# Turning queries, keys and outputs on the matmul engine instead of with transposing transfers, and three VectorE sums moved

## The chip, the cores and the metric

The kernel runs on one core of one Trainium2 chip. The metric is the device time of one execution in microseconds (us), as the median of several runs. One execution was also recorded by the hardware profiler, and all views quoted below come from that recording.

The engines are named as in the profile: PE is the matmul engine (TensorE) and PEld its weight loads, DVE is VectorE, ACT is ScalarE, POOL is GpSimd, and SP is SyncE, which here only issues transfers. A small q behind a name (SPq, PEq) is that engine's sequencer.

## What is computed

Causal attention with 16 extra "beacon" keys and values ahead of each sequence, followed by two matrix products with a leaky ReLU between them:

```python
B, H, S, D = 8, 8, 576, 64            # beacons: 16; d_model 512, d_ff 2048
k_all = concat([beacon_k, k], axis=2); v_all = concat([beacon_v, v], axis=2)
scores = 1/sqrt(D) * q @ k_all^T       # causal over k, beacons always visible
a = softmax(scores)
attn = a @ v_all
x = attn.transpose(0, 2, 1, 3).reshape(B*S, H*D)      # 4608 tokens x 512
h = x @ w_in                                          # 512 -> 2048
out = maximum(0.01*h, h) @ w_out                      # 2048 -> 512
```

Inputs and output are float32; the kernel's matmuls take bf16.

## The kernel before

**Pairs.** The 64 heads are worked on as 32 pairs `g` of two heads (NG = 32, four pairs to a batch). For a pair the kernel needs q and k with the head dimension on the partitions (tiles `qT`, `kT`, 128 x 576: two heads of 64). It then computes transposed scores on PE into PSUM, exponentials on ACT into `aT`, causal triangles on POOL (L289), and on PE the product with the values, `value` (L359), in two halves. DVE divides by the row sums (L388, L389) and writes `x_nat`, tokens on the partitions. For the first product of the second stage `x_nat` has to be turned again, into `xT`.

**How things are turned.** For the first eight pairs, q and k are turned on PE (`t_q`, L243) and copied from PSUM by DVE or ACT (L249). For pairs 8 to 31, POOL loads q and k with a cast (`load_natural`, L171, tiles `q_nat`, `k_nat`, 96 partitions by 6 blocks of 128), and `turn_pair` turns each with one transposing transfer issued by SP (L179). The outputs of pairs 0 to 3, 5, 6, 7 and 31 are turned by `x_transposes` (five PE transposes at L405, one copy at L410). Those of pair 4 and of pairs 8 to 30 are turned by `x_turn`: two or three transposing transfers on SP (L417, L422, L425).

**Second stage.** The 4608 tokens are cut into nine chunks of 512. `moe1` (L442, called by `up`) makes one 128 x 512 block of the hidden layer; ACT applies the leaky ReLU (L450) into `gT`. `moe2` (L525, called by `down`) multiplies by `w_out` in seven products instead of eight (a Strassen-like scheme), each of two tiles of eight matmuls. For these products DVE builds sums of token blocks (`token_sums`, queued in the list `due` and issued one at a time by `add_due`, L801), sums of weight blocks once (`weight_sums`, L468 to L474), and adds the products (L551 for chunk 0, L588 later). The last two chunks also use seven products in the first matrix (`in_round`, L679).

**Order.** Every engine runs its queue in program order, and the order is written by hand. The eight first pairs follow strings of steps given to `run` (for example `T8` turns pair 8, `x7` turns the output of pair 7, `t1` is the second weight sum, `d` is one `down`). From pair 8 (FIRST) on, a list of events with positions in units of a pair is sorted: loads `N` at g - 3.25 and g - 2.95, `T` at g - 1.75, a `block` of scores (three tiles of 512 columns, running over pair limits) every 0.92 units, `value` at g + 2.25 and 0.37 later (0.2 earlier for the last pair of a batch), the turn of the output 0.01 after that. Between the events `fill` issues `up` and `down` so that the work of the second stage is spread evenly.

**PSUM.** Four banks (`ps_one`, tag "one") go round among the `up` blocks, the products of `down`, the value products, the first score tile of a block (two banks) and the tiles `tp` of PE transposes. A bank comes free when ACT or DVE has read it.

Of the kernel before, what the change touches and what calls it, by code (L numbers as in the profile page):

```python
# [9 lines left out]
BF16 = mybir.dt.bfloat16  # L10
# [5 lines left out]
def kernel(  # L16
# [11 lines left out]
    nc = tc.nc  # L28

    B, H, S, D = q.shape  # L30
# [5 lines left out]
    NPAIR = H // 2  # L36
# [9 lines left out]
    NKB = 5  # L46
# [17 lines left out]
    NR = 96  # L64
# [77 lines left out]
    qk_raw, nat, qk = {}, {}, {}  # L142
# [31 lines left out]
            )  # L174
        nat.setdefault(g, []).append(t)

    def turn_pair(g):
        for which, t in enumerate(nat.pop(g)):
            nc.sync.dma_start_transpose(  # L179
                out=operand(g, which).rearrange("c (t r) -> c t r", r=NR),  # L180
                in_=t.rearrange("r t h d -> r (t h d)"),
            )

    def load_beacon_k(b0, b1, eng):
        eng.dma_start(out=bk_raw[:, b0:b1], in_=beacon_k[b0:b1].rearrange("b h n d -> (h n) b d"))
# [33 lines left out]
    def operand(g, which):  # L219
        qk.setdefault(g, [None, None])  # L220
        if which == 0:
            qk[g][0] = headpool.tile([128, S], BF16, name="qT", bufs=5)
            return qk[g][0]
        qk[g][1] = k_bufs[g % NK]
        return qk[g][1][:, NB : NB + S]
# [170 lines left out]
    def x_at(b):  # L396
        assert b < XR or done1[0] >= NF * -(-((b - XR + 1) * S + 48) // 512)
        return b % XR * S
# [10 lines left out]
            )  # L409
        copy(out=xT[:, hp, x_at(b) : x_at(b) + S], in_=ps[:, 0:S])  # L410

    def x_turn(g):
        b, hp = divmod(g, NPAIR)
        x_nat, _ = xs.pop(g)
        t1 = NKB if b < B - 1 else NKB - 1
        dst = xT[:, hp, x_at(b) : x_at(b) + 112 + (t1 - 1) * 128]
        nc.sync.dma_start_transpose(  # L417
            out=dst[:, 112:].rearrange("c (t r) -> c t r", r=128),
            in_=x_nat[:, 1:t1].rearrange("r t e d -> r (t e d)"),
        )  # L420
        if t1 < NKB:
            nc.sync.dma_start_transpose(  # L422
                out=xT[:, hp, x_at(b) + S - 80 : x_at(b) + S], in_=x_nat[0:80, t1].rearrange("r e d -> r (e d)")
            )
        nc.sync.dma_start_transpose(  # L425
            out=dst[:, 0:112], in_=x_nat[0:112, 0].rearrange("r e d -> r (e d)")
        )

    gT = {}

    def moe1(i, fc):
# [30 lines left out]
    def weight_sums(part):  # L462
        b11, b12 = w_out_sb[:, 0:HF, 0:HD], w_out_sb[:, 0:HF, HD:DM]
        b21, b22 = w_out_sb[:, HF:NF, 0:HD], w_out_sb[:, HF:NF, HD:DM]
        t1, t2, t4 = (w_sum[:, i] for i in range(3))
        tt = nc.vector.tensor_tensor
        if part == 0:
            tt(out=t1, in0=b12, in1=b11, op=SUB)  # L468
        elif part == 1:
            tt(out=t2, in0=b22, in1=t1, op=SUB)  # L470
        elif part == 2:
            tt(out=b12, in0=b22, in1=b12, op=SUB)
        else:
            tt(out=t4, in0=b21, in1=t2, op=SUB)  # L474
# [42 lines left out]
    def moe2(i, n2):  # L517
        n, tile = (PRODUCTS if i else FIRST_PRODUCTS)[n2 // 2], n2 % 2
        apart = i == NCH - 1 and n2 >= 10
        if tile == 0 or apart:  # L520
            banks["p"] = one_bank()
        acc = banks["p"]
        lo = 0 if apart else tile * HD
        for fc in range(HF):
            nc.tensor.matmul(  # L525
                out=acc[:, lo : lo + HD],
                lhsT=left(i, n, fc, tile),
                rhs=right(n, fc),
                start=(lo == 0 and fc == 0),
                stop=(fc == HF - 1),  # L530
                skip_group_check=True,
            )
        if apart:
            combine(i, n, acc[:, 0:HD], (tile, tile + 1))
        elif tile == 1:
            (combine if i else combine_first)(i, n, acc, (0, 2))
# [7 lines left out]
    def combine_first(i, n, acc, tiles):  # L544
        def part(name, new=False):
            if new:
                parts[name] = opool.tile([128, 512], FP32, name=name, bufs=1)
            return parts[name]

        def add(to, x, y):  # L550
            nc.vector.tensor_tensor(out=to, in0=x, in1=y, op=ADD)  # L551

        if n in (1, 3, 5):
            nc.scalar.copy(out=part({1: "p1", 3: "p5", 5: "p4"}[n], True), in_=acc)
        elif n == 2:
            add(part("u3", True), acc, part("p1"))
            store(i, 0, 0, tiles, part("u3"))
        elif n == 6:
            add(part("u2", True), acc, part("p1"))
            weight_sums(2)  # L560
        elif n == 7:
            add(part("p1"), acc, part("u2"))
            weight_sums(3)
            p1, p4, p5, u2 = (part(name) for name in ("p1", "p4", "p5", "u2"))

            def rest():
                add(p5, p5, p4)
                add(p5, p5, u2)
                store(i, 0, 1, tiles, p5)
                add(part("u3", True), p1, p4)  # L570
                store(i, 1, 1, tiles, part("u3"))

            late.append((done1[0] + done2[0], rest))
        elif n == 4:
            add_late(True)
            add(part("p4"), acc, part("p1"))
            store(i, 1, 0, tiles, part("p4"))
# [221 lines left out]
    def add_due(n=1):  # L799
        while due and n:  # L800
            nc.vector.tensor_tensor(**due.pop(0)[1])  # L801
            n -= 1

    def add_all(i):
        while due and due[0][0] == i:
            add_due()
# [20 lines left out]
    def down():  # L827
        add_late()
        add_due()
        if at2[1] == 4:  # L830
            add_all(at2[0])
        moe2(*at2)
        done2[0] += 1
        at2[1] += 1
        if at2[1] == ND(at2[0]):
            at2[:] = at2[0] + 1, 0
        turn[0] = 0
# [40 lines left out]
    def run(steps):  # L878
        for step in steps.split():
            op, a = step[0], [int(x) for x in step[1:].split(".")] if step[1:] else []  # L880
            if op == "s":
                score(*a)
            elif op == "m":
                mask(*a)
            elif op == "v":
                value(*a)
            elif op == "e":
                value_ahead(*a)
            elif op == "x":
                finish(*a)  # L890
            elif op == "l":
                load_qk(*a)
            elif op == "V":
                load_v_cast(*a)
            elif op == "N":
                load_natural(*a)
            elif op == "T":
                turn_pair(a[0])
            elif op == "y":
                x_turn(a[0])  # L900
            elif op == "q" or op == "k":
                t_q(a[0], 0 if op == "q" else 1, (dve, act)[a[1] if len(a) > 1 else 0])
            elif op == "b":
                beacon_columns(a[0], (dve, act, pool)[a[1]])
            elif op == "u":
                up()
            elif op == "d":
                down()
            elif op == "w":
                unused(*a)  # L910
            elif op == "W":
                unused_ahead(*a)
            elif op == "i":
                load_w_in(a[0])
            elif op == "o":
                load_w_out(a[0])
            elif op == "t":
                weight_sums(a[0])
            else:
                raise ValueError(step)  # L920
# [11 lines left out]
    with order:  # L932
# [16 lines left out]
        run("w2.384 s1.0 m1.0 q2 s1.1 k2 w2.384 s1.2 m1.1 w2.384 s1.3 m1.2 W0.0.4 s2.0 m2.0 W0.0.4 s2.1 W0.0.6 q3 l5.0 l5.1 s2.2 k3 w4.384 v0.0 m2.1 s2.3 i1 m2.2 W0.1.4 s3.0 m3.0 v1.0 s3.1 v0.1 s3.2 v1.1 m3.1 l6.0 l6.1 s3.3 x0.1 m3.2")  # L949
        run("v2.0 V1.0 V1.1 q4 v2.1 x1 k4.1 v3.0 v3.1 x2.1 s4.0 s4.1 x3 m4.0 V1.2 V1.3 V1.4 l7.0 l7.1 u u s4.2 s4.3 q5 k5 m4.1 m4.2 u o0 u")  # L950
        load_beacon_k(2, B, nc.gpsimd)
        run("s5.0 s5.1 m5.0 u u u s5.2 s5.3 q6 k6 m5.1 m5.2 o1 u u s6.0 s6.1 m6.0 u v4.0 u v4.1 y4 N8.0 N8.1 u s6.2 s6.3 q7 k7 m6.1 m6.2 u")
        cast_beacon_k(2, B, nc.gpsimd.tensor_copy)
        run("u v5.0 u v5.1 N9.0 s7.0 s7.1 m7.0 d x5 v6.0 v6.1 t0 T8 d s7.2 s7.3")
        beacon_transposes(2, B)
        run("m7.1 m7.2 N9.1 u b8.2 b9.2 b10.2 b11.2 x6 v7.0 T9 v7.1 d d d N10.0 N10.1 d V2.0 V2.1 x7 t1 T10")


        FIRST = 2 * NPAIR
# [24 lines left out]
        for g in range(FIRST, NG):  # L984
            if g > FIRST + 2:
                events.append((g - 3.25, 0, run, ("N%d.0" % g,)))
                events.append((g - 2.95, 0, run, ("N%d.1" % g,)))
            if g > FIRST + 2:
                events.append((g - 1.75, 0, run, ("T%d" % g,)))
            if g > FIRST + 3:  # L990
                events.append((g - 2.5, 0, run, ("b%d.2" % g,)))
            at = g + (2.05 if g % NPAIR == NPAIR - 1 else 2.25)
            events.append((at, 3, value, (g, 0)))
            events.append((at + 0.37, 4, value, (g, 1)))
            if g < NG - 1:
                events.append((at + 0.38, 5, x_turn, (g,)))
        for m in range((TILES + 2) // 3):
            events.append((FIRST + (0.4 if m else 0.6) + 1536 / COLS * m, 2, block, (m,)))
        ends = [FIRST]
# [60 lines left out]
```

## Time and profile before

| | |
|---|---|
| time, median of 3 runs | 327.32 us (327.24 to 327.57) |
| profiled execution, its own time | 325.4 us |
| its span, first to last instruction | 323.5 us |
| PE busy | 313.3 us (97%) |
| DVE, ACT, POOL busy | 174.6, 205.1, 186.5 us |
| mean granted PE clock | 0.999 |
| transposing transfers on SP | 24 + 24 (q, k) and 51 (outputs) |

An instruction's line in these views tells engine, source line, operation, the tile written and read, shapes, how often, busy time, mean length, and the idle time of the engine before it with what ended it. Matmuls are pipelined, so the length of one matmul (say 273 ns for 256 columns) is longer than the distance to the next (109 ns); where the cost of a group on PE matters, the distance from its start to the start of the next group is the thing to read.

### The profile page before, as it was taken

What the parts mean: (1) busy time and instruction counts of PE and PEld (TensorE: products, weight loads), DVE (VectorE), ACT (ScalarE), POOL (GpSimd) and SP (SyncE); (2) the same over time, 40 slices, a digit from 0 to 9 for tenths busy, and PEclk for the clock granted to TensorE, in tenths of its full rate; (3) what the DMA queues carried; (4) which work ended last, traced back from release to release, by engine and by line L of the source; (5) the groups of instructions that cost most, each with busy time, mean ns of one, the idle gap of its engine ahead of it and who ended that gap; (6) DMA issues with size and microseconds to landing.
All of it is one profiled execution on the core that took longest, in us unless ns stands there. A gap on an engine that the chain in (4) does not pass through costs nothing.

```text
span 323.5 us, 8812 instructions
## 1 busy us (share of the span) xinstructions
PE 313.3 (97%) x3517; PEld 223.6 (69%) x3542; DVE 174.6 (54%) x352; ACT 205.1 (63%) x349; POOL 186.5 (58%) x354
## 2 busy tenths in 40 slices
PE   8999997989999999999999999999999999999995
PEld 5584576655588557855788888656875688688784
DVE  3473388455355244444543454425464689577954
ACT  4969863569856786478746874687458546455510
POOL 8994979989997787659875977666221000000000
PEclk9999999999999999999999999999999999999999
DMA  8999999999999999999999999999422101200113
GB/s 139 142 209 175 140 202 128 166 142 208 145 137 164 189 179 126 123 179 98 133 167 183 122 120 129 184 140 113 55 76 84 26 0 34 77 23 0 67 65 131
DMA packets 155769, 39.79 MB, mean 123 GB/s; under 512 B 142368, under 2 KB 153504, under 8 KB 155728
## 3 DMA queue, kind: packets, MB, share of 16 engines
q0 software_dynamic: 99824, 18.54, 86.0%
q1 hardware_dynamic: 55632, 20.62, 38.5%
q8 instruction: 27, 0.44, 0.6%
q14 instruction: 14, 0.11, 0.1%
q10 hardware_dynamic: 272, 0.07, 0.1%
HBM read 37.22 MB, written 9.44 MB: 144 GB/s over the span
## 4 chain that ended last, share of the span: by engine, by line
PE 80%; DMA 10%; ACT 3%; DVE 2%; POOL 1%; issue 1%; SPq 0%; ACTq 0%
PE acc L442 26%; PE acc L525 21%; PE sc L525 11%; PE av L359 7%; PE sc L314 5%; DMA kT<-k_nat 5%; PE acc L679 5%; DMA w_out_sb<-in_moe_w_out_dram 4%; PE sc L267 2%; DMA gsum<-in_k_dram 1%; ACT aT L333 1%; PE tp L243 1%; POOL aT L289 1%; ACT aT L276 1%; ACT gT L450 1%
## 5 line engine op out<-in xcount | busy, mean ns | idle before, releaser
L442 PE MATMUL acc<-xT,w_in_sb 128*128 128x512 bf16 (+1 forms) x535 | 116.3, 354 | 1.3
L450 ACT ACTIVATE gT<-acc 128x512 bf16<-128x512 f32 x124 | 70.8, 624 | 33.0 <-PE acc L442 32.6
L289 POOL TENSOR_SCALAR_AFFINE_SELECT aT<-aT 128x256 bf16<-128x256 bf16 (+2 forms) x160 | 61.6, 415 | 51.2 <-ACT aT L329 30.7
L442 PEld LDWEIGHTS <-w_in_sb 128*128 128x128 bf16 x560 | 51.6, 98 | 43.0 <-issue 2.7
L525 PEld LDWEIGHTS <-gT 128*128 128x128 bf16 x576 | 54.6, 98 | 12.0 <-issue 4.0
L333 ACT ACTIVATE aT<-sc 128x1024 bf16<-128x1024 f32 (+3 forms) x64 | 51.7, 891 | 0.0
L388 DVE RECIPROCAL rec<-av 128x6 f32<-128x6 f32 (+1 forms) x64 | 11.9, 186 | 64.8 <-PE av L359 64.3
L525 PEld LDWEIGHTS <-gsum 128*128 128x128 bf16 x432 | 40.9, 98 | 8.4 <-DVE gsum L801 1.2
L329 ACT ACTIVATE aT<-sc 128x512 bf16<-128x512 f32 (+3 forms) x64 | 28.9, 520 | 21.1 <-PE sc L314 20.4
L359 PEld LDWEIGHTS <-aT 128*128 128x128 bf16 (+1 forms) x960 | 36.7, 98 | 7.9 <-issue 0.6
L359 PE MATMUL av<-v_aug,aT 128*128 128x65 bf16 (+1 forms) x960 | 39.0, 194 | 0.0
L525 PE MATMUL acc<-w_out_sb,gT 128*128 128x256 bf16 x288 | 34.9, 273 | 1.2 <-DMA w_out_sb<-in_moe_w_out_dram 0.6
L171 POOL DMA_DIRECT2D k_nat<-in_k_dram x48 | 34.8, 731 | 1.9 <-DMA v_aug<-in_v_dram 0.8
L214 POOL DMA_DIRECT2D v_aug<-in_v_dram x40 | 34.2, 862 | 2.9 <-DMA w_in_sb<-in_moe_w_in_dram 2.8
L171 POOL DMA_DIRECT2D q_nat<-in_q_dram x48 | 34.8, 730 | 0.7 <-issue 0.5
L389 DVE TENSOR_TENSOR x_nat<-av,rec 128x384 bf16<-128x384 f32 (+1 forms) x64 | 31.4, 491 | 2.2
L276 ACT ACTIVATE aT<-sc 128x1024 bf16<-128x1024 f32 (+3 forms) x32 | 25.9, 875 | 1.9 <-PE sc L267 1.9
L525 PE MATMUL acc<-w_sum,gsum 128*128 128x256 bf16 x192 | 23.9, 273 | 0.0
L314 PE MATMUL sc<-qT,kT 64*128 64x80 bf16 (+22 forms) x384 | 22.3, 250 | 0.7 <-DMA kT<-k_nat 0.6
L801 DVE TENSOR_TENSOR gsum<-gT 128x1024 bf16<-128x1024 bf16 x18 | 12.7, 705 | 15.7 <-ACT gT L450 15.7
L314 PEld LDWEIGHTS <-kT 64*128 64x128 bf16 x384 | 12.8, 94 | 11.2 <-issue 7.0
L591 ACT COPY p<-acc 128x512 f32<-128x512 f32 x15 | 9.1, 604 | 16.0 <-PE acc L525 16.0
(98 smaller groups left out, 332.5 us busy)
## 6 DMA issues: line engine op xcount, KB each, us to landing
out_dram<-p SPq DMA_DIRECT2D x25, 256.0 KB, 3.6
q_nat<-in_q_dram POOLq DMA_DIRECT2D x48, 72.0 KB, 5.4
k_nat<-in_k_dram POOLq DMA_DIRECT2D x48, 72.0 KB, 5.4
v_aug<-in_v_dram POOLq DMA_DIRECT2D x24, 128.0 KB, 6.5
out_dram<-u SPq DMA_DIRECT2D x9, 256.0 KB, 4.7
w_in_sb<-in_moe_w_in_dram POOLq DMA_DIRECT2D x2, 1024.0 KB, 12.3
w_out_sb<-in_moe_w_out_dram POOLq DMA_DIRECT2D x2, 1024.0 KB, 11.5
gsum<-in_q_dram POOLq DMA_DIRECT2D x8, 144.0 KB, 6.0
```

The costliest lines, as they stand in the source:

```text
L171: nc.gpsimd.dma_start(out=t[:, :, par], in_=(q, k)[which][b, 2 * hp + par].rearrange("(t p) d -> p t d", p=NR),)
L214: nc.gpsimd.dma_start(out=dst[lo : ROWS[c], c, :, 0:D], in_=v[b, :, OFF[c] : OFF[c] + n].rearrange("h p d -> p h d"),)
L276: nc.scalar.activation(out=aT[:, :, c0 : c0 + w], in_=sc[:, :, 0:w], func=AF.Exp, scale=0.125)
L289: nc.gpsimd.affine_select(out=view, in_=view, compare_op=ALU.is_ge, fill=0.0, base=128 - n if lo == 0 else 0, channel_multiplier=-1, patte ...
L314: nc.tensor.matmul(out=(sc[par] if apart else sc[:, par])[:, at : at + b - a], lhsT=kT[ps_, c * 128 : (c + 1) * 128], rhs=qT[ps_, q0 : q0 ...
L329: nc.scalar.activation(out=probs[g][:, par, lo:hi], in_=sc[par][:, at : at + hi - lo], func=AF.Exp, scale=0.125)
L333: nc.scalar.activation(out=probs[g][:, :, lo:hi], in_=sc[:, :, at : at + hi - lo], func=AF.Exp, scale=0.125)
L359: nc.tensor.matmul(out=avv[:, n, 0 : D + 1], lhsT=aT[0 : ROWS[c], par, a0 : a0 + 128], rhs=va[0 : ROWS[c], c, 2 * hp + par, :], start=(c = ...
L389: nc.vector.tensor_tensor(out=x_nat[:, t0:t1].rearrange("p t e d -> p (t e) d"), in0=avv[:, :, 0:D], in1=rec[:, n0:n1, None].to_broadcast( ...
L442: nc.tensor.matmul(out=acc[:, lo:hi], lhsT=w_in_cols(fc, j), rhs=xT[:, j, x0 : x0 + hi - lo], start=(j == 0), stop=(j == NJ - 1), skip_gro ...
L450: nc.scalar.activation(out=gT[i][:, fc, :], in_=acc, func=AF.Prelu, alpha=0.01)
L525: nc.tensor.matmul(out=acc[:, lo : lo + HD], lhsT=left(i, n, fc, tile), rhs=right(n, fc), start=(lo == 0 and fc == 0), stop=(fc == HF - 1) ...
```

## The change

`turn_pair` and `x_turn` go, and with them all 99 transposing transfers. `turn_natural(g, which)` takes the place of the first: six PE transposes of 96 x 128 into a PSUM bank and one DVE copy into `qT` or `kT`. For the outputs of pair 4 and of pairs 8 to 30 `x_transposes` is used, with the copy on DVE. Positions: `T` is now two events, q at g - 1.15 and k at g - 0.85; the output is turned 0.75 instead of 0.38 units after the first value half. `T8` moves to the end of the strings, `T9` and `T10` into the events. Three sums on VectorE stand earlier: the weight sum of L472 directly behind that of L470 (in `t1`), the weight sum of L474 behind product 6 instead of product 7, and at the second product of chunk 0 two more token sums are issued ahead of the product.

```diff
-    def turn_pair(g):
-        for which, t in enumerate(nat.pop(g)):
-            nc.sync.dma_start_transpose(
-                out=operand(g, which).rearrange("c (t r) -> c t r", r=NR),
-                in_=t.rearrange("r t h d -> r (t h d)"),
+    def turn_natural(g, which):
+        t = nat[g][which]
+        ps = ps_one.tile([128, 1024], BF16, name="tp", tag="one")
+        for n in range(S // NR):
+            nc.tensor.transpose(
+                ps[:, n * NR : (n + 1) * NR], t[:, n].rearrange("r h d -> r (h d)"), ident[0:NR, 0:NR]
             )
+        nc.vector.tensor_copy(out=operand(g, which), in_=ps[:, 0:S])
...
-    def x_turn(g):
...
@@ weight_sums
         elif part == 1:
             tt(out=t2, in0=b22, in1=t1, op=SUB)
-        elif part == 2:
             tt(out=b12, in0=b22, in1=b12, op=SUB)
         else:
             tt(out=t4, in0=b21, in1=t2, op=SUB)
@@ combine_first
         elif n == 7:
             add(part("p1"), acc, part("u2"))
-            weight_sums(3)
@@ down
         if at2[1] == 4:
             add_all(at2[0])
+        elif at2 == [0, 2]:
+            add_due(2)
         moe2(*at2)
@@ the strings of the first pairs
-   ... "v4.0 u v4.1 y4 N8.0 N8.1 u s6.2" ...
+   ... "v4.0 u v4.1 N8.0 N8.1 u x4 s6.2" ...
-   ... "v6.0 v6.1 t0 T8 d s7.2 s7.3"
+   ... "v6.0 v6.1 t0 d s7.2 s7.3"
-   "m7.1 m7.2 N9.1 u b8.2 b9.2 b10.2 b11.2 x6 v7.0 T9 v7.1 d d d N10.0 N10.1 d V2.0 V2.1 x7 t1 T10"
+   "m7.1 m7.2 N9.1 u b8.2 b9.2 b10.2 b11.2 x6 v7.0 v7.1 d d d N10.0 N10.1 d V2.0 V2.1 x7 t1 T8.0 T8.1"
@@ the events
-            if g > FIRST + 2:
-                events.append((g - 1.75, 0, run, ("T%d" % g,)))
+            if g > FIRST:
+                events.append((g - 1.15, 0, run, ("T%d.0" % g,)))
+                events.append((g - 0.85, 0, run, ("T%d.1" % g,)))
...
-                events.append((at + 0.38, 5, x_turn, (g,)))
+                events.append((at + 0.75, 5, x_transposes, (g, dve)))
```

More of the change, by code (lines that the diff above doesn't have):

```diff
@@ L410, in x_transposes @@
         copy(out=xT[:, hp, x_at(b) : x_at(b) + S], in_=ps[:, 0:S])
-    def x_turn(g):
[L413 to L427, printed above, removed]
     gT = {}
@@ L897, in run @@
             elif op == "T":
-                turn_pair(a[0])
-            elif op == "y":
-                x_turn(a[0])
+                turn_natural(*a)
             elif op == "q" or op == "k":
@@ L951 @@
         load_beacon_k(2, B, nc.gpsimd)
-        run("s5.0 s5.1 m5.0 u u u s5.2 s5.3 q6 k6 m5.1 m5.2 o1 u u s6.0 s6.1 m6.0 u v4.0 u v4.1 y4 N8.0 N8.1 u s6.2 s6.3 q7 k7 m6.1 m6.2 u")
+        run("s5.0 s5.1 m5.0 u u u s5.2 s5.3 q6 k6 m5.1 m5.2 o1 u u s6.0 s6.1 m6.0 u v4.0 u v4.1 N8.0 N8.1 u x4 s6.2 s6.3 q7 k7 m6.1 m6.2 u")
         cast_beacon_k(2, B, nc.gpsimd.tensor_copy)
-        run("u v5.0 u v5.1 N9.0 s7.0 s7.1 m7.0 d x5 v6.0 v6.1 t0 T8 d s7.2 s7.3")
+        run("u v5.0 u v5.1 N9.0 s7.0 s7.1 m7.0 d x5 v6.0 v6.1 t0 d s7.2 s7.3")
         beacon_transposes(2, B)
-        run("m7.1 m7.2 N9.1 u b8.2 b9.2 b10.2 b11.2 x6 v7.0 T9 v7.1 d d d N10.0 N10.1 d V2.0 V2.1 x7 t1 T10")
+        run("m7.1 m7.2 N9.1 u b8.2 b9.2 b10.2 b11.2 x6 v7.0 v7.1 d d d N10.0 N10.1 d V2.0 V2.1 x7 t1 T8.0 T8.1")
         FIRST = 2 * NPAIR
```

## The prediction

> **What bounds the kernel now.** I read the page first: which engine is full, and what ends last.
>
> ```profile
> PE 313.3 (97%) x3517; PEld 223.6 (69%) x3542; DVE 174.6 (54%) x352; ACT 205.1 (63%) x349; POOL 186.5 (58%) x354
> DMA  8999999999999999999999999999422101200113
> PE 80%; DMA 10%; ACT 3%; DVE 2%; POOL 1%; issue 1%; SPq 0%; ACTq 0%
> ```
>
> PE is busy for 97% of the span and holds 80% of the chain that ended last. The transfer engines are full too, up to slice 28 (about 230 us), and own 10% of the chain. Two questions decide: is PE really full, or does it only look so because matmul ends are modelled; and how long does it stand still for those transfers? For the first, the windows by stage (after the stretch and its length: busy time and count of PE, PEld, DVE, ACT, POOL, the granted clock, the transfers' share and GB/s), and the timeline of PE:
>
> ```profile
> 60.00:110.00 50.00, 47.77 (x527) 31.63 (x531) 24.47 (x45) 35.97 (x65) 46.19 (x88) 1.00 1.87 165
> 110.00:160.00 50.00, 49.54 (x515) 32.11 (x517) 23.04 (x47) 35.49 (x64) 37.06 (x67) 1.00 1.71 143
> 160.00:210.00 50.00, 49.95 (x614) 41.50 (x613) 22.65 (x46) 32.37 (x57) 35.94 (x70) 1.00 1.54 149
> ```
> ```profile
> 132.32 0.53 PE L359 MATMUL av<-v_aug,aT 128*128 128x65 bf16 x12
> 132.69 1.04 PE L525 MATMUL acc<-w_out_sb,gT 128*128 128x256 bf16 x8
> 133.57 1.04 PE L525 MATMUL acc<-w_sum,gsum 128*128 128x256 bf16 x8
> 134.53 0.83 PE L314 MATMUL sc<-qT,kT 64*128 64x320 bf16 x16
> ```
>
> From start to start, eight matmuls of 256 columns take 133.57 - 132.69 = 0.88 us, 0.43 ns a column, and the next group follows at once. The clock is 1.00. PE is full in earnest: what is added to it there lengthens the run by as much, and only time in which it stands still can be won. For the second question, all that PE's matmuls waited for (total us, times, longest):
>
> ```profile
> PE acc L525 <- DVE w_sum L474: 1.1, 1, 1.1
> PE av L843 <- DVE blank L935: 1.1, 1, 1.1
> PE acc L525 <- DVE gsum L801: 0.9, 1, 0.9
> PE acc L525 <- DMA w_out_sb<-in_moe_w_out_dram: 0.6, 1, 0.6
> PE sc L314 <- DMA kT<-k_nat: 0.6, 1, 0.6
> ```
>
> The chain books 5% on the transfer `kT<-k_nat`, 7.47 us of it at 77.17, yet PE lost 0.6 us to it: during those 7 us it had other work, and the chain only tells which arrival came last. (L843 is the start, before 2 us.) A further wait of L525, on L472, adds 0.2. So 99 transposing transfers cost PE almost nothing, although they keep the transfer engines full.
>
> **The change part by part.** *Added on PE.* 24 pairs x 2 operands x 6 = 288 transposes for q and k, and 24 outputs x 5 = 120: 72 batches, each of 576 columns (6 x 96, or 112 + 3 x 128 + 80). The profile has the very batch, eight times, at L405:
>
> ```profile
> 22.23 0.42 PE L405 MATMUL tp<-ident,x_nat 112*128 112x112 bf16 x5
> 22.57 0.47 PE L243 MATMUL tp<-ident,gsum 64*64 64x64 bf16 x18
> ...
> 46.35 0.42 PE L405 MATMUL tp<-ident,x_nat 112*128 112x112 bf16 x5
> 46.61 1.08 PE L359 MATMUL av<-v_aug,aT 128*128 128x65 bf16 x30
> ```
>
> Start to start it takes 0.34 in the first pair of lines and 0.26 in the second; the eight are 0.27, 0.34, 0.35, 0.28, 0.26, 0.26, 0.26, 0.26, mean 0.285. At 0.43 ns a column 576 columns come to 0.25. Six pieces in place of five change little: value matmuls of only 65 columns follow each other at 0.55 / 18 = 31 ns, 3 ns over their columns. I take the mean, which includes small waits of the crowded early part: 72 x 0.285 = 20.5 us. Bounds: 72 x 0.25 = 18.0 and 72 x 0.35 = 25.2. One batch, the output of pair 4, falls near 42 us, ahead of a wait for `w_out` (0.6) that would absorb it: 0.3, left inside the rounding.
>
> The Trainium skill ("TensorE: Matmul & The Clock Gate", Part 4: PE-mode transpose) speaks against the change: it gives about 275 ns for one 128 x 128 transpose inside a kernel, and says that transposes do not engage the full clock. By that price, as an estimate, 408 transposes would be 112 us. The row here agrees on the length of one (217 ns), but five of them pass in 0.26 us because they are pipelined, and the granted clock stays at 1.00, so the sum goes by the row.
>
> *Added on DVE.* 72 copies of 128 x 576 from PSUM. The same copy at L410 takes 456 ns: 72 x 0.456 = 32.8 us. DVE has about 24 of 50 us busy in the middle, and one pair takes about (257 - 60) / 24 = 8.2 us there, to which 3 x 0.456 = 1.4 are added: about 5.3 of 9. DVE doesn't become the bound. Its price is the bank: a copy that stands behind a sum (0.69 us) holds one of four banks longer, and PE's next-but-three tile waits for it. The banks' other users need at least 0.87 us of PE each, so three of them cover 2.6 us, more than a sum and a copy (1.15). Cost nothing, with that cover; without it, up to 0.69 a batch, of which I keep 5 us for the range. Work queued behind a DVE copy that waits for its transposes: reciprocals and sums, all of which DVE would issue for later PE work anyway.
>
> *Waits moved onto PE.* Before, SP waited for the loads of q and k; now PE does, in order. Loads are issued at g - 3.25, the first transposes stand at g - 1.15, 2.1 units or about 17 us later; the median load lands in 5.4 us, the slowest in 14.3. Only early pairs are close: SP's transfer for the keys of pair 11 waited for their load until 71.9, and by its place just ahead of the block at 71.5 PE would turn them at about 71. From 0 to 1.5 us; with less traffic on the queues I take 0. The turn of an output now makes PE wait for L389, which is 0.38 units, 3 us, behind its value matmuls: covered. SP's queue keeps only the stores, which nobody waits for.
>
> *Removed and moved.* The wait for `kT<-k_nat` goes (0.6). The sum L474 gets a product's time more, its wait goes (1.1), as does that for L472 (0.2); the token sums ahead of product 2 remove the wait for L801 (0.9). Together 2.9; each of the four begins only when the last matmul's modelled length (0.27) is over, 0.16 after its true pitch (0.11), so 4 x 0.16 more: 3.5 us won. Nothing else can be won late: past 257 us PE has no wait.
>
> What takes the place of these waits is seen in DVE's timeline at the end of the first pairs:
>
> ```profile
> 57.41 0.46 DVE L410 COPY xT<-tp 128x576 bf16<-128x576 bf16 x1 [1.23 <-PE tp L405]
> 57.78 1.22 DVE L470 TENSOR_TENSOR w_sum<-w_out_sb,w_sum 128x2048 bf16<-128x2048 bf16 x1
> ```
>
> Behind L470 there will be 1.22 us of L472 and then the copies of pair 8, until about 60.6. Their tiles hold two banks and pair 9's a third. PE has 0.8 us of transposes from 57.2 and one product (1.75) in the fourth bank, so it comes at 59.75 to a bank that is free at 60.6: 0.9 us lost (0 to 2).
>
> *Sum.* 325.4 (profiled) + 20.5 - 3.5 + 0.9 = 343.3. The median of the runs stands 1.9 above the profiled execution (327.3 to 325.4), so 345.2 us, 5.5% slower.
>
> **The rivals.** *Banks and copies (slower still).* If copies wait behind DVE's sums often enough, each batch stalls PE. For it: DVE's sums come four in a row from 77.5 us, and ACT's exponentials (1.05 us each) already hold banks. Against it: in 197 us PE waited for no bank for more than 0.2 us. Half of the batches at 0.3 us would add 11: 356.
>
> *The transfers were the brake (faster).* One mechanism: with the transposing queue (38.5% of 16 engines with the stores) gone, loads land earlier and PE's waits for arrivals end. For it: 10% of the chain. Against it: PE's waits for transfers are 1.2 us in the list, all its removable waits 3.5. It decides only if a batch cost PE less than 3.5 / 72 = 49 ns, where the rows show 260 and more. Were a batch 30 ns, as one value matmul is, the time would be 327.3 + 2.2 - 3.5 = 326.0.
>
> *The batches hide in PE's gaps (the change does less than it says).* The span has 323.5 - 313.3 = 10.2 us without a matmul. If 8 of these took up batches, the time were 337. Against it: about 5 of them lie before 10 us and after 320, where no batch is.
>
> **How the numbers follow.** My forecast (340 to 350) gets 0.72, the bank case (350 to 360) 0.20, the gaps (333 to 340) 0.05, the faster case 0.03. The low end is 327.3 + 18.0 - 3.5 - 1.0 (the wait for `w_out` and the listed ones under 0.5) = 340.8, so 340; the high end is 327.3 + 25.2 - 3.5 + 2 + 1 of the 5 us kept for banks, 352. A measurement of this kernel tells 0.2% from no change. Faster by more than that 0.03, within it 0.01, slower 0.96.
>
> **What would show it.** Right: PE's groups at L405 and in the new function with some 448 transposes, each batch 0.26 to 0.29 us to the next group; no DMA_TRANSPOSE rows; PE's busy time up by about 20; no waits on L474, L472 and `kT`; the stage from pair 8 to 31 (197 us) some 17 longer; DVE's copies of 128 x 576 about 0.46 each, some 207 us busy. Wrong: waits of PE for `q_nat` or `k_nat`, for DVE copies or for banks that add up to more than 3 us; batches under 0.2 us; or a mean granted clock well under 1.

## The result and the profile after

The changed kernel takes 349.12 us (median of 4 runs; 327.28 before in the same series): ratio 1.0662, 95% interval 1.0624 to 1.0699. The forecast was 345.2, range 340 to 352: right in direction and inside the range, 3.9 us short. Measured again later beside another kernel its ratio was 1.0696 (1.0652 to 1.0739). The profiled execution took 349.16, its span is 347.5: 24.0 more than the span before. Undisturbed executions of the kernel before reach from 324 to 329 us and some executions of most kernels are over 1.5% longer, so the ratios and times below are of undisturbed executions only, while the profiles of x_on_pe, qk_on_pe and pe_twice are of longer ones, whose extra 6 us lie almost all ahead of the turn of pair 7's output (57.0 us in the changed kernel, 62.6 to 63.1 there). Differences are judged by ratios to the kernel before and their intervals; 1% is 3.3 us.

The page after, the lines that answer to those shown of before:

```profile
PE 333.8 (96%) x3920; PEld 243.8 (70%) x3950; DVE 202.6 (58%) x424; ACT 206.1 (59%) x349; POOL 187.2 (54%) x354
DMA  8999999996997996779968895889111000100113
q1 hardware_dynamic: 9984, 9.73, 8.5%
PE 83%; ACT 6%; DVE 3%; DMA 3%; POOL 2%; issue 1%; ACTq 0%; POOLq 0%
```

PE is 20.5 us busier (313.3 to 333.8) and nearly as full as before (97%, now 96%). From the turn of pair 7's output to the first product that is written to a score tile, when the pairs are done, the kernel took 200.2 us before (56.95 to 257.18) and takes 223.5 now (57.00 to 280.55). Nearly all of the loss lies there, 23.3 us where some 17 had been forecast. The transfer queue that carried the transposing transfers and the stores falls from 38.5% to 8.5% of the 16 engines, and the loads of q and k land sooner; the page before and the page after:

```profile
q1 hardware_dynamic: 55632, 20.62, 38.5%
q_nat<-in_q_dram POOLq DMA_DIRECT2D x48, 72.0 KB, 5.4
```
```profile
q_nat<-in_q_dram POOLq DMA_DIRECT2D x48, 72.0 KB, 3.3
```

The last number of a load's line is the median time to landing in us. The kernel as a whole did not become faster for it. The waits of PE's matmuls (total, times, longest):

```profile
PE tp L407 <- DVE x_nat L391: 1.6, 5, 0.6
PE tp L181 <- DVE qT L184: 1.5, 1, 1.5
PE av L828 <- DVE blank L918: 1.1, 1, 1.1
PE av L361 <- DMA v_aug<-in_v_dram: 0.9, 1, 0.9
PE acc L427 <- ACT gT L435: 0.7, 2, 0.4
PE av L361 <- ACT p L574: 0.7, 1, 0.7
PE acc L509 <- DVE gsum L784: 0.6, 1, 0.6
```

The waits on the weight sums and on `kT` are gone; the one on the token sums shrank from 0.9 to 0.6. In their place stand waits that the kernel before did not have: for `x_nat`, for a copy of pair 8 (`qT`), and for banks that ACT had still to read (`p`, and `gT` ahead of L427 and, 0.3 us more, ahead of L316). The wait for `v_aug` lies at 17 us, ahead of any changed instruction, and the profile of the same kernel measured again doesn't have it. The wait for `qT`, in PE's timeline (start, length, engine, line, what, count, and in brackets the idle time before and what ended it):

```profile
57.26 0.42 PE L181 MATMUL tp<-ident,q_nat 96*128 96x96 bf16 x6
57.52 0.42 PE L181 MATMUL tp<-ident,k_nat 96*128 96x96 bf16 x6
57.84 0.42 PE L181 MATMUL tp<-ident,q_nat 96*128 96x96 bf16 x6
58.09 1.04 PE L509 MATMUL acc<-w_sum,gsum 128*128 128x256 bf16 x8
60.61 0.41 PE L181 MATMUL tp<-ident,k_nat 96*128 96x96 bf16 x6 [1.48 <-DVE qT L184]
```

A batch takes 0.26 from start to start, as forecast. Three tiles `tp` and one product fill the four banks; the keys of pair 9 then need the bank of pair 8's queries, whose copy stands on DVE behind both weight sums:

```profile
57.84 1.22 DVE L455 TENSOR_TENSOR w_sum<-w_out_sb,w_sum 128x2048 bf16<-128x2048 bf16 x1
58.97 1.22 DVE L456 TENSOR_TENSOR w_out_sb<-w_out_sb 128x2048 bf16<-128x2048 bf16 x1
60.10 0.45 DVE L184 COPY qT<-tp 128x576 bf16<-128x576 bf16 x1
```

And the wait for `x_nat`, PE's timeline again:

```profile
158.18 0.72 PE L361 MATMUL av<-v_aug,aT 128*128 128x65 bf16 x18
158.74 0.42 PE L181 MATMUL tp<-ident,q_nat 96*128 96x96 bf16 x6
158.99 0.33 PE L407 MATMUL tp<-ident,x_nat 112*128 112x112 bf16 x3
159.63 0.27 PE L407 MATMUL tp<-ident,x_nat 128*128 128x128 bf16 x2 [0.32 <-DVE x_nat L391]
```

Only one batch, 0.25 us, stands between the second value half and the turn of the output, so the last two row blocks wait for the division on DVE; the batch takes 0.75 (to 159.74).

### The profile page after: what moved, and what is told of

Same layout as the page of the kernel before. It is cut to its first block, busy times and chain, and to the rows that moved or that the text cites. A ratio compares the mean times of both kernels' runs of the same rounds, so it can differ in the third digit from the quotient of the medians.

```text
span 347.5 us, 9479 instructions
## 1 busy us (share of the span) xinstructions
PE 333.8 (96%) x3920; PEld 243.8 (70%) x3950; DVE 202.6 (58%) x424; ACT 206.1 (59%) x349; POOL 187.2 (54%) x354
## 4 chain that ended last, share of the span: by engine, by line
PE 83%; ACT 6%; DVE 3%; DMA 3%; POOL 2%; issue 1%; ACTq 0%; POOLq 0%
PE acc L427 28%; PE acc L509 20%; PE sc L509 11%; PE av L361 8%; PE sc L316 6%; PE acc L662 4%; ACT aT L335 3%; DMA v_aug<-in_v_dram 3%; PE tp L181 2%; PE tp L407 2%; ACT gT L435 2%; PE sc L269 1%; DVE x_nat L391 1%; POOL gsum L158 1%; ACT aT L331 1%
## 5 line engine op out<-in xcount | busy, mean ns | idle before, releaser
L427 PE MATMUL acc<-xT,w_in_sb 128*128 128x512 bf16 (+1 forms) x530 | 119.0, 354 | 2.5 <-ACT gT L435 0.7
L291 POOL TENSOR_SCALAR_AFFINE_SELECT aT<-aT 128x256 bf16<-128x256 bf16 (+2 forms) x160 | 62.4, 417 | 74.4 <-ACT aT L331 48.5
L427 PEld LDWEIGHTS <-w_in_sb 128*128 128x128 bf16 x560 | 50.6, 98 | 40.3 <-issue 4.2
L509 PE MATMUL acc<-w_out_sb,gT 128*128 128x256 bf16 x288 | 36.1, 273 | 0.0
L509 PE MATMUL acc<-w_sum,gsum 128*128 128x256 bf16 x192 | 24.6, 273 | 0.0
L316 PE MATMUL sc<-qT,kT 64*128 64x80 bf16 (+22 forms) x384 | 22.0, 250 | 0.3 <-ACT gT L435 0.3
L412 DVE COPY xT<-tp 128x576 bf16<-128x576 bf16 x30 | 13.7, 456 | 13.5 <-PE tp L407 13.4
L316 PEld LDWEIGHTS <-kT 64*128 64x128 bf16 x384 | 12.8, 94 | 9.0 <-issue 5.7
```

The lines of the kernel that those rows point to most:

```text
L291: nc.gpsimd.affine_select(out=view, in_=view, compare_op=ALU.is_ge, fill=0.0, base=128 - n if lo == 0 else 0, channel_multiplier=-1, patte ...
L316: nc.tensor.matmul(out=(sc[par] if apart else sc[:, par])[:, at : at + b - a], lhsT=kT[ps_, c * 128 : (c + 1) * 128], rhs=qT[ps_, q0 : q0 ...
L427: nc.tensor.matmul(out=acc[:, lo:hi], lhsT=w_in_cols(fc, j), rhs=xT[:, j, x0 : x0 + hi - lo], start=(j == 0), stop=(j == NJ - 1), skip_gro ...
L509: nc.tensor.matmul(out=acc[:, lo : lo + HD], lhsT=left(i, n, fc, tile), rhs=right(n, fc), start=(lo == 0 and fc == 0), stop=(fc == HF - 1) ...
```

## The experiments

The theory: PE is full, so a batch costs its columns at PE's pitch, about 0.26; transfers were hidden; only standing time can be won. The rivals: the transfers were the brake; or banks and DVE's copies, not columns, carry the price.

**What turning is worth at all (no_turn).**

```diff
     def turn_natural(g, which):
-        t = nat[g][which]
...
-        nc.vector.tensor_copy(out=operand(g, which), in_=ps[:, 0:S])
+        nc.vector.tensor_copy(out=operand(g, which), in_=dummy)
@@ x_transposes, for the 24 outputs
+            nc.vector.tensor_copy(out=xT[:, hp, x_at(b) : x_at(b) + S], in_=dummy)
+            return
```

> The changed kernel in which those 24 pairs are not turned at all: a DVE copy of a constant tile writes qT, kT and xT in place of the transposes, with no transfer either, so the output is not attention's. It prices transposing transfers and transposes against nothing. Theory (the transfers were hidden): before less PE's removable waits, 327.3 - 2 for the sums - 1 for kT = 324, between 322 and 326; the distance to the changed kernel, 25 us, is 72 batches of 0.26 (18.7) and their waits. Rival (transfers were the brake and the change gives part of what it wins back): 318 or less.

Measured: 324.89, ratio 0.9952 (0.9933 to 0.9971). Without these transfers and transposes the kernel wins some 1.6 us (0.9 to 2.2). That is all that 99 transposing transfers, plus the places of the three sums, cost before, net of the 72 copies that this kernel still makes on DVE; the rival needed 318. The same work on PE costs 349.1 - 324.9 = 24.2 us, or 23.2 and 24.4 by the ratios of the changed kernel's two measurements. The page shows the transfer engines less than 90% busy in more slices than before, and PE as full as ever:

```profile
PE 315.0 (97%) x3542; PEld 224.2 (69%) x3542; DVE 194.1 (60%) x425; ACT 205.1 (63%) x349; POOL 186.2 (58%) x354
DMA  7999999999999997779977998997120001200113
```

**The sums alone (sums_only).**

```diff
         elif part == 1:
             tt(out=t2, in0=b22, in1=t1, op=SUB)
-        elif part == 2:
             tt(out=b12, in0=b22, in1=b12, op=SUB)
@@ combine_first, n == 7
-            weight_sums(3)
@@ down
+        elif at2 == [0, 2]:
+            add_due(2)
```

> The kernel before with the three moved sums alone; all 99 transposing transfers stay. Theory (only time in which PE stands still can be won): the waits of PE on L474 (1.3 us by starts) and L472 (0.3) go, the one on the token sums shrinks from 1.1 to 0.8 as it did in the changed kernel; 1.5 to 2.5 us faster than before, 325 to 326. Rival (the sums sat beside other work and a wait takes the place of each): no change, 327.

Measured: 326.1, ratio 0.9984 (0.9954 to 1.0013), from 12 executions: 0.5 us faster, a third of the least that the theory gave, and not told from no change; the interval's low end, 1.5 us, is still the theory's least. The profile is nearer to the rival: the stretch from the turn of pair 7's output to the first product in a score tile takes 200.0 us, 200.2 before. The two waits on the weight sums are gone, but PE stands ahead of the next score blocks:

```profile
60.45 0.85 PE L314 MATMUL sc<-qT,kT 64*128 64x512 bf16 x12 [0.33 <-issue]
64.38 0.89 PE L314 MATMUL sc<-qT,kT 64*128 64x48 bf16 x15 [0.25 <-ACT gT L450]
70.24 0.72 PE L314 MATMUL sc<-qT,kT 64*128 64x256 bf16 x10 [0.30 <-POOL aT L289]
```

Three new waits, 0.9 us together, of which the kernel before had none. For two of them ACT and POOL were the next to be late; for the first the profile names nobody ("issue").

**The two halves (x_on_pe, qk_on_pe).** Both hold the moved sums.

```diff
@@ x_on_pe, from the kernel with the sums alone
-   ... "v4.1 y4 N8.0 N8.1 u s6.2"
+   ... "v4.1 N8.0 N8.1 u x4 s6.2"
-                events.append((at + 0.38, 5, x_turn, (g,)))
+                events.append((at + 0.75, 5, x_transposes, (g, dve)))
@@ qk_on_pe, from the changed kernel
-   ... "v4.1 N8.0 N8.1 u x4 s6.2"
+   ... "v4.1 y4 N8.0 N8.1 u s6.2"
-                events.append((at + 0.75, 5, x_transposes, (g, dve)))
+                events.append((at + 0.38, 5, x_turn, (g,)))
```

> The three sums and the outputs of 24 pairs turned on PE (24 batches of 5 transposes, copies on DVE); queries and keys by transfers as before. Theory (pitch plus the wait for x_nat): 24 x 0.26 = 6.3 us of PE plus 2.5 us of waits for L389's result on top of the kernel with the sums alone, so about 325.5 + 8.8 = 334. Rival (banks: the tiles of the transposes only jam when all three a pair are there): 325.5 + 6.3 = 332.

> The changed kernel with the outputs turned by transfers again (51 transposing transfers, at their old places); queries and keys on PE. Theory: 48 x 0.26 = 12.5 us of PE, 1.5 us of the jam behind the weight sums, about 1.7 us of bank waits, less 1 us of waits for kT: 325.5 + 14.7 = 340. Rival (banks jam only with all three tiles a pair): 325.5 + 12.5 + 1.5 - 1 = 338.5, and the two parts together then fall short of the whole change (349) by more than 3 us.

Measured: x_on_pe 335.0, ratio 1.0273 (1.0237 to 1.0309); qk_on_pe 337.8, ratio 1.0355 (1.0320 to 1.0391). Over the sums alone (0.9984) that is 2.89% and 3.71%, 9.5 and 12.1 us; together 21.6, against 1.0662 - 0.9984 = 6.78%, 22.2 us, for the whole. The halves add up within the intervals (over 1 us on each ratio), so the rival's jam of more than 3 us from three tiles a pair isn't seen. 24 outputs cost 0.39 us each, 48 operands 0.25: the outputs are dear (x_on_pe lies above its theory's 334, and above the rival's 332). Its profile has the reason, which the changed kernel's has too (1.6 us, 5 times):

```profile
PE tp L405 <- DVE x_nat L389: 2.5, 6, 0.6
```

For qk_on_pe the time lies below theory (340) and rival (338.5) both. That the parts add up is settled by the sum; the theory's waits for banks were set too high.

**Columns or surroundings (pe_twice, copies_twice).** From the changed kernel:

```diff
@@ pe_twice
-        for n in range(S // NR):
+        for n in [*range(S // NR)] * 2:
-        for t, (q0, rows) in enumerate(QT):
+        for t, (q0, rows) in [*enumerate(QT)] * (2 if g == 4 or 8 <= g < 31 else 1):
@@ copies_twice
-        nc.vector.tensor_copy(out=operand(g, which), in_=ps[:, 0:S])
+        dst = operand(g, which)
+        for _ in range(2):
+            nc.vector.tensor_copy(out=dst, in_=ps[:, 0:S])
@@ and likewise the copies into xT
```

> The changed kernel with every added batch of transposes made twice into the same bank (72 batches and 408 transposes more on PE, nothing else added). Theory (a batch costs its columns at PE's pitch): 72 x 0.25 = 18.0 us, 349.1 + 18 = 367, perhaps 1 us less where a wait covers the first copy. Rival (a batch's price is the changes of kind and the waits around it, which a second batch behind the first doesn't pay): under 10 us, 358 or less.

> The changed kernel with the copy behind each added batch made twice on DVE (72 x 0.456 = 32.8 us more DVE work, every bank held 0.46 us longer). Theory (copies are covered; DVE is busy for 58%): 1 to 4 us slower, of which 1.4 lie in the jam at 59 us where three copies follow the weight sums; 350 to 353. Rival (banks and DVE's queue carry the price of the change): 10 us or more, 359 and up.

Measured: pe_twice 362.7 and 362.9, ratio 1.1129 (1.1058 to 1.1199): 4.3 to 4.7% over the two measurements of the changed kernel, 14 to 15 us, with over 2 us of uncertainty. The second batch is itself as dear as the first one:

```profile
180.23 0.67 PE L181 MATMUL tp<-ident,q_nat 96*128 96x96 bf16 x12
180.74 0.92 PE L407 MATMUL tp<-ident,x_nat 112*128 112x112 bf16 x10
```

Twelve transposes in 0.51 us. The expected 18 is missed by 3 to 4, in part because the second batches cover more waits than allowed for: the wait for pair 8's copy falls from 1.5 to 0.8, those for `x_nat` from 1.6 to 0.8 in the list, 1.5 us in all; the rest of the shortfall is not traced. The rival (under 10) is out.

copies_twice: 352.57, ratio 1.0816 (1.0764 to 1.0868), 4 to 5 us more by the ratios for 32.8 us of DVE. In its profile the wait for pair 8's copy grows from 1.5 to 2.1 and bank waits behind ACT from 0.7 to 1.1. Copies are covered for the most part, as forecast; the upper end of the expected 1 to 4 was a little low.

**Two places (t8_first, both_places, changed_again, both_again).**

```diff
-   "... x7 t1 T8.0 T8.1"
+   "... x7 T8.0 T8.1 t1"
@@ both_places and both_again also
-                events.append((at + 0.75, 5, x_transposes, (g, dve)))
+                events.append((at + 1.0, 5, x_transposes, (g, dve)))
```

> The changed kernel with one step moved: the turns of pair 8 stand ahead of the weight sums of t1, so that their copies don't wait behind 2.4 us of sums. Theory: PE's wait for the copy of pair 8 at 59 us (1.5 us) goes, 347.6. Rival (the wait moves on to the sums' users or to pair 9's tile): 349.

> As t8_first, and the turn of an output 0.25 units (2 us) later. Theory: PE's five or six waits for the last rows of x_nat (2.3 us together over a plain batch of 0.26) go as well, 345.3, which leaves about 72 x 0.26 = 18.7 and 1 to 2 us of bank waits over the kernel without turning (324.9). Rival (the batch waits elsewhere, or the later turn makes moe1 wait for xT): 347 or more.

> The changed kernel unaltered, beside both_again on one chip, since the kernels with moved places were measured on another chip than it. Theory and rival agree: 1.066 of before, 348 to 349.5.

> The two moved places (turns of pair 8 ahead of the weight sums, outputs turned 2 us later) again, beside the changed kernel on one chip. Theory (the 1.5 us wait for pair 8's copy and some 2 us of waits for x_nat are worth their length): 3 to 4 us below the changed kernel, 345.5. Rival (most of each comes back as a wait for ACT's copies or banks, as the sums' gain did): less than 1.5 us below it, 347 or more.

Measured: t8_first 347.65, ratio 1.0666 (1.0632 to 1.0700). The wait for `qT` is no longer in its list and its span is 345.8, but against the changed kernel (1.0662 on another chip, 1.0696 in a later series) the intervals can't tell its 1.5 us. both_places 345.4, ratio 1.0607 (1.0554 to 1.0660), with the same difficulty. Side by side on one chip: changed_again 348.5 (1.0696, 1.0652 to 1.0739), both_again 345.1 (1.0590, 1.0556 to 1.0625). 3.4 us, as the theory said (3 to 4). PE's waits in both_again:

```profile
PE av L828 <- DVE blank L918: 1.1, 1, 1.1
PE tp L407 <- ACT p L574: 0.7, 1, 0.7
PE acc L509 <- DVE gsum L784: 0.6, 1, 0.6
PE acc L509 <- ACT p L574: 0.5, 1, 0.5
PE acc L509 <- ACT gT L435: 0.5, 1, 0.5
```

`x_nat` and `qT` are gone from it. What is left over the kernel without turning is 345.1 - 324.9 = 20.2 us, of which 72 x 0.26 = 18.7 are the batches themselves. The other 1.5 is a remainder; the three waits for ACT in this list (1.7 together) are of its size. Whether another order would remove them was not tried.

**A faster kernel by earlier transfers (early, sums_early).** From the kernel before and from sums_only:

```diff
-                events.append((g - 3.25, 0, run, ("N%d.0" % g,)))
+                events.append((g - 3.65, 0, run, ("N%d.0" % g,)))
@@ likewise N%d.1 from 2.95 to 3.35, T from 1.75 to 2.25, b from 2.5 to 2.9
```

> The kernel before with the loads of queries and keys 0.4 units and their transposing transfers 0.5 units (4 us) earlier, nothing else. Theory (of the transfers only the late arrival of kT stops PE, about 1 us by starts): that wait goes, 326.0 to 326.5. Rival (PE then meets the next wait at once, as it did when the sums moved): no change, 327.

> The three sums and the earlier loads and transposing transfers together. Theory: the moved sums (-0.8 measured) and the wait for kT (-1) add up to 325.2, near the kernel without any turning (324.9), and faster than both kernels. Rival: the earlier transfers crowd the loads of the values and win nothing: 326.3.

Measured: ratios 1.0072 (1.0015 to 1.0130) and 1.0107 (1.0069 to 1.0145), 2.4 and 3.5 us. Both theories fall; both kernels are slower. The second one's rival named the mechanism but not its size: more loads of queries and keys now stand ahead of the loads of values on POOL's queue. The last load of one batch's values, in sums_only and in sums_early:

```profile
90.63 0.76 POOL L214 DMA_DIRECT2D v_aug<-in_v_dram  x1
```
```profile
95.37 0.73 POOL L214 DMA_DIRECT2D v_aug<-in_v_dram  x1
```

In sums_early this load takes 8.0 us to land, and PE waits for it. PE's timeline and the windows around it (stretch, length, busy times of PE, PEld, DVE, ACT, POOL, granted clock, transfers):

```profile
103.39 0.49 PE L359 MATMUL av<-v_aug,aT 80*128 80x65 bf16 x6 [2.65 <-DMA v_aug<-in_v_dram]
```
```profile
95.00:100.00 5.00, 5.00 (x66) 4.16 (x64) 1.99 (x4) 2.98 (x5) 4.99 (x11) 1.00 1.88 111
100.00:104.00 4.00, 1.25 (x21) 0.99 (x20) 1.12 (x4) 0.00 (x0) 4.00 (x10) 0.88 2.36 148
104.00:108.00 4.00, 4.00 (x36) 2.77 (x35) 1.90 (x4) 1.23 (x3) 1.48 (x3) 0.70 1.69 233
```

The kernel `early` has the same wait, 2.95 us in its profiled execution (332.3 us). The wait for `kT` did not go either (1.4 us in two in sums_early, 0.8 in two in sums_only, 0.6 before). So here loads that came earlier pushed another load later. Loads and transposing transfers were moved together, so what the transposing transfers alone would do at an earlier place is not shown. No kernel that computes the attention is faster than the one before beyond the measurement.

## Why the prediction was right, and where it was short

- *PE is full, so columns cost time: right.* Batches have a median of 0.26 from start to start, for q and k as for outputs, 72 x 0.26 = 18.7. Beside it stand 23.2 to 24.4 (no_turn), 21.6 (the halves), both with the waits around the batches, and 14 to 15 for a second set (pe_twice), which covers waits in part.
- *The sum, split by no_turn: short in both of its parts.* The kernel without turning prices what can be won: 1.6 where the forecast had 3.5. The distance from there to the changed kernel prices the turning: 23.2 by the ratios of the two, where the forecast had 20.5 + 0.9 = 21.4. The two misses, 1.9 and 1.8, are the missing 3.9.
- *The batch term, 20.5 from the mean of eight: too small.* Over the profile the 72 batches take 24.4 from their start to the next group, 0.34 each. The 5.7 over 18.7 are waits inside and just behind them, which the eight early batches show only in part. The measured time is inside the range because the upper end gave every batch the slowest of the eight, 0.35, which the mean of 0.34 all but reached; with the eight's mean the upper end would have been 347.
- *"The turn of an output makes PE wait for L389, 3 us behind its value matmuls: covered": wrong.* Units of a pair in the list of events are no distance on PE: 0.38 units were taken for 3 us, and in the trace the turn that waits has one batch of q between itself and its second value half (four times) or nothing (once). These five batches take 0.65 to 1.0, 2.5 us over the plain ones.
- *The jam behind the weight sums: right in kind, 0.9 forecast, 1.5 in the list.* I had the second product meet the held bank; it was the keys of pair 9, which stand one tile earlier.
- *3.5 us won from removed waits: too much.* The waits on the weight sums and on `kT` went, but the wait on the token sums kept 0.6 of its 0.9, and other waits came: the sums alone gave 0.16%, about 0.5 us by the ratio and not told from nothing, and no_turn 1.6.
- *Copies and banks: small, but not nothing.* I had set their cost at nothing, and more than 3 us of waits for DVE copies and banks as a sign of being wrong. The list has 1.5 for the copy of pair 8 and 1.7 for banks that ACT had still to read: 3.2, just over it.
- *DVE is not the bound: right.* 202.6 us busy (forecast 207), copies 0.45 each; doubling them costs 4 to 5 of 32.8.
- *Loads: right.* No wait for a load of `q_nat` or `k_nat` is in the list.
- *Profiles against medians.* The medians lie 21.8 us apart, the two profiled executions 23.8, of which 0.9 is the wait for `v_aug` at 17 us. So times in the two lists can't be set against the medians closer than some 2 us.
- *Resolution.* I took 0.2% for what a measurement can tell from no change; the intervals here are 0.2 to 0.7% to each side.
- *The rivals.* Transfers as the brake: refuted by no_turn. Batches in PE's gaps (337): refuted by the time. Banks: present, with waits of some 3 us, not 11.
- *The skill's price.* By the figure of the Trainium skill ("TensorE: Matmul & The Clock Gate", Part 4: PE-mode transpose) the estimate was 112 us; the measured cost is 23 to 24. One transpose is some 217 ns long here, a fifth less than the page's 275, and transposes in a row overlap: twelve pass in 0.51 us. With 448 of them among the matmuls the mean granted clock was 0.999; no run here shows a long stretch of transposes alone.

## What to carry to other kernels

On a full matmul engine, count what a move adds there in columns times pitch and set it against what PE really stands still for, not against a transfer's share of the chain: 99 transposing transfers, on transfer engines that were 90% busy and more for most of the run, cost about 1.6 us with the places of three sums, their replacement 23 to 24. A removed wait need not be worth its length: in sums_only 0.9 us of new waits came for 1.3 removed, while in both_again 3.1 us of removed waits gave 3.4. So look which engine is late next before pricing it. If work must move to PE, place it by what stands in PE's queue between producer and turn, and put copies that free banks ahead of long sums on the copying engine: the two places here together were worth 3.4 us.

## What the runs showed of the hardware that was not expected

In sums_early PE stood 2.65 us for one load, and the granted clock, 1.00 ahead of it, was 0.88 in the 4 us around the wait and 0.70 in the 4 us after it. In windows of 1 us it falls to half and comes back:

```profile
102.00:103.00 1.00, 0.00 (x0) 0.00 (x0) 0.00 (x0) 0.00 (x0) 1.00 (x4) 1.00 2.89 148
103.00:104.00 1.00, 0.61 (x8) 0.55 (x8) 0.09 (x1) 0.00 (x0) 1.00 (x2) 0.51 2.63 132
104.00:105.00 1.00, 1.00 (x7) 0.69 (x6) 0.52 (x2) 0.00 (x0) 1.00 (x3) 0.50 1.72 163
105.00:106.00 1.00, 1.00 (x6) 0.71 (x5) 0.00 (x0) 0.38 (x1) 0.48 (x1) 0.50 1.76 211
106.00:107.00 1.00, 1.00 (x11) 0.62 (x9) 0.73 (x2) 0.20 (x1) 0.00 (x0) 0.78 1.59 290
107.00:108.00 1.00, 1.00 (x20) 0.75 (x17) 0.65 (x1) 0.65 (x2) 0.00 (x0) 1.00 1.72 267
```

The granted clock is the third number from the end. PE's timeline behind the wait:

```profile
103.69 1.90 PE L524 MATMUL acc<-w_sum,gsum 128*128 128x256 bf16 x8
105.37 1.56 PE L524 MATMUL acc<-w_out_sb,gsum 128*128 128x256 bf16 x8
106.87 0.83 PE L314 MATMUL sc<-qT,kT 64*128 64x272 bf16 x16
```

These two groups of eight matmuls take 1.68 and 1.50 us from start to start instead of 0.88, so the wait cost 1.4 us more than its length. In `early` the wait of 2.95 us was likewise followed by a clock of 0.50, in the three windows from 105 to 108 us. The waits of 1.5 us in the changed kernel and of 2.1 us in copies_twice, both for the copy of pair 8, left the clock at 1.00. The Trainium skill ("TensorE: Matmul & The Clock Gate", section "Why this matters for your kernels") warns of idle gaps of more than about 3 us between bursts. Here a slightly shorter one was enough: with these four waits the limit lies between 2.1 and 2.65 us, if the length alone decides, which no run here shows.
